# Down-projection and output projection with the weights as the standing operand, results turned by transposing DMAs

## The chip, the cores and the metric

The kernel runs on one core of one Trainium2 chip. The metric is the device time of one execution, in microseconds (us). The kernel before was run three times.

## What is computed

The kernel computes a layer norm, then two branches on its result, and joins them:

```python
xn = layernorm(x)                          # x: 2048 tokens x 640, bf16
q, k, v = split(xn @ wqkv)                 # 32 heads of 20
p = softmax(q @ k.T / sqrt(20))            # per head 2048 x 2048
s = concat_heads(p @ v) @ wo               # 640 x 640
h = sigmoid(xn @ w_gate) * (xn @ w_up)     # 640 -> 1728
g = silu(h @ w_down)                       # 1728 -> 640
out = x + s * g
```

## The kernel before

Tokens lie in 16 tiles of 128, or in four chunks (`c`) of 512. Heads go in eight groups of four (`g`). One group on one chunk of queries is a **block**; there are 32 blocks, and the last eight alternate groups 6 and 7 over chunks 0 to 3. A block has 64 score jobs, each of 128 keys by 512 queries for one head.

**Scores and exponentials.** A *fill* (line 889) multiplies two to four scores at once into PSUM: two into the pair `scA`, the others into single banks `bk` (three exist). ScalarE (ACT) takes the exponential of a pair (`pt`, 1024 wide) or of a bank (`px`, 512 wide), all through line 82. VectorE (DVE) computes exponentials too: an integer conversion out of a bank (`iv`, line 1327) and, for up to four together, three passes (`pb`, lines 1019, 1022, 1025). The attention sum (line 926) adds into `oacc`.

**The other matrix work** shares the three banks `bk`. It is cut into items of small steps, all through `cols` (line 473): four matmuls side by side, each with 32 columns of a standing operand. The gated unit's hidden values are `hT` (hidden x tokens). `mk_down` (line 719) multiplies them by `wd`: here `hT` stands and `wd` streams, so one item is 128 tokens by 320 outputs, 14 steps, eight items a chunk. ACT takes a tanh (`td`, 320 wide), DVE makes the silu (`gqs`, line 740), and for chunks 0 to 2 it is stored to DRAM (`gq_dram`, line 742); chunk 3 stays in SBUF (`gql`).

**The output projection** of chunks 0 to 2 (`mk_out`, line 773) multiplies the normalized attention `oU` by `wo`, `oU` standing: 128 tokens by 320, five steps, 24 items. DVE multiplies by the silu loaded again (`otmp`, line 795), GpSimd (POOL) adds `x` in two parts (line 800), and each token tile is stored (line 802). `load_out` (line 764) loads `x` and the silu into one of three areas of `xnT` that are free by then. Chunk 3 is finished in a tail written by hand (lines 1053 to 1136), whose first products (`early`, line 1045) may fill banks before attention is done.

**Normalization of a block** goes through DRAM: DVE copies `oacc` (line 959), SyncE (SP) issues `ld` and `lt`, DVE takes the reciprocal (`rt`, line 969), SP issues `rd` and four `rl`, POOL multiplies (lines 979, 984), SP issues the pieces of `oU` (lines 1009, 1011).

**What sets the order.** On PE, ACT, DVE and POOL the order is written by a planner, the loop from line 1231: it walks its own clock with fixed costs (0.2133 for a step 512 wide, 0.14 for one of `mk_down`), gives a fill to PE when ACT is about to run dry, and otherwise attention sums or steps of items, as far as their due times ask. DVE's exponentials are claimed at a fill, when DVE is not far behind and a bank is free; so the split of the 2048 jobs between ACT and DVE follows from the plan. POOL's adds wait in a list and are placed by `beat` beside DVE instructions that read PSUM. The order on SP's queue is not the planner's: it is settled when the program is built. All engines execute their queue in order.

Of the kernel before, what the change touches and what calls it, by code (L numbers as in the profile page):

```python
# [51 lines left out]
def kernel(  # L52
# [38 lines left out]
    persist = ctx.enter_context(tc.tile_pool(name="persist", bufs=1))  # L91
    wk = ctx.enter_context(tc.tile_pool(name="wk", bufs=2))

    gq_dram = dram.tile([S, D], FP32, name="gq_dram", tag="gqd", bufs=1)
# [373 lines left out]
    def mark(*e):  # L468
        return lambda t: ev_at.__setitem__(e, t)
# [194 lines left out]
    def mk_gu(c, kf, at):  # L664
        st = {}
        fs = fsz[kf]
        k2, ko = divmod(kf, 2)

        def alloc0():
            if (c, k2) not in wgu_tiles:  # L670
                load_wgu(c, k2)
            st["g"] = misc_ps()

        def alloc1():
            st["u"] = misc_ps()
            if ko == 0:
                n = c * NK2 + k2 + 1
                if n < NQC * NK2:
                    load_wgu(*divmod(n, NK2))

        def mm(key, i, kd):
            w = wgu_tiles[(c, k2)]
            cols(st[key], w[:, i, kd, ko * P:ko * P + P], xnT[:, c, kd, :], kd == 0, kd == KD - 1)

        def th():
            st["t"] = w2.tile([P, QC], BF16, tag="tnh", bufs=2, name="tnh")
            act_imm(st["t"][0:fs, :], st["g"][0:fs, :], ACT.Tanh, 0.5)

        def ev():
            return nc.vector.scalar_tensor_tensor(out=hT[0:fs, kf, :], in0=st["t"][0:fs, :], scalar=1.0,  # L690
                                                  in1=st["u"][0:fs, :], op0=ALU.add, op1=ALU.mult)

        def mm2(kd):
            cols(st["g"], wgu_tiles[(c, k2)][:, 0, kd, P:2 * P], xnT[:, c, kd, :], kd == 0, kd == KD - 1)

        def th2():
            st["t"] = w2.tile([P, QC], BF16, tag="tnh", bufs=2, name="tnh")
# [15 lines left out]
    def gq_last(t4):  # L713
        if len(gq_l) == t4 // 2:
            w = w2.tile([P, 2, KD, 2 * P], BF16, tag="wgu", bufs=2, name="gql")
            gq_l.append(w.rearrange("p i k f -> p (i k f)").bitcast(FP32))
        return gq_l[t4 // 2][:, t4 % 2 * D:(t4 % 2 + 1) * D]

    def mk_down(c, t4, h, at):
        st = {}  # L720
        tt = 4 * c + t4

        def alloc():
            st["ps"] = misc_ps()

        def mm(kf):
            cols(st["ps"][:, 0:HD], hT[:, kf, t4 * P:(t4 + 1) * P], wd[:, kf, h * HD:(h + 1) * HD],
                 kf == 0, kf == NFT - 1)

        def th():  # L730
            st["td"] = w2.tile([P, HD], BF16, tag="td", bufs=2, name="td")
            act_imm(st["td"], st["ps"][:, 0:HD], ACT.Tanh, 0.25)

        def ev():
            if c == NQC - 1:
                return nc.vector.scalar_tensor_tensor(out=gq_last(t4)[:, h * HD:(h + 1) * HD], in0=st["td"], scalar=1.0,
                                                      in1=st["ps"][:, 0:HD], op0=ALU.add, op1=ALU.mult)
            flush("o")
            gqs = w2.tile([P, HD], FP32, tag="gqs", bufs=3, name="gqs")
            ins = nc.vector.scalar_tensor_tensor(out=gqs, in0=st["td"], scalar=1.0, in1=st["ps"][:, 0:HD],  # L740
                                                 op0=ALU.add, op1=ALU.mult)
            nc.sync.dma_start(out=gq_dram[tt * P:(tt + 1) * P, h * HD:(h + 1) * HD], in_=gqs)
            return ins
        return Item([("PE", alloc, [(0.14, lambda kf=kf: mm(kf)) for kf in range(NFT)]),
                     ("ACT", 0.32, th), ("DVE", 0.40, ev, "free", mark("d", c, t4, h))], at, pre=[("h", c, kf) for kf in range(NFT)])


    FL, FG, FK = (NG - 1) * GC, (NG - 2) * GC, (KD - 1) * P
    FM = FG + 2 * DH
# [11 lines left out]
                                in1=rq.broadcast_to((P, n, GH, DH)), op=ALU.mult)  # L761
        return onq

    def load_out(tt):
        if tt in out_tiles:
            return
        o2 = xfl[:, tt % 3 * KD * QC:tt % 3 * KD * QC + 3 * D]
        flush("o")
        out_tiles[tt] = (o2[:, 0:D], o2[:, D:3 * D].bitcast(FP32))
        nc.sync.dma_start(out=out_tiles[tt][0], in_=x2[tt * P:(tt + 1) * P, :])  # L770
        nc.sync.dma_start(out=out_tiles[tt][1], in_=gq_dram[tt * P:(tt + 1) * P, :])

    def mk_out(tt, h, at):
        st = {}

        def alloc():
            if h == 0:
                load_out(tt)
                if (tt + 1) % 4:
                    load_out(tt + 1)  # L780
            st["ps"] = misc_ps()

        def mm(kd):
            hs = slice(h * HD, (h + 1) * HD)
            cols(st["ps"][:, 0:HD], oU[:, kd, tt * P:(tt + 1) * P], wo[:, kd, hs], kd == 0, kd == KD - 1)

        def ev():
            xr, gqr = out_tiles[tt]
            sl = slice(h * HD, (h + 1) * HD)
            while sum(x[1] == "o" for x in pool_q) > 2:  # L790
                x = next(x for x in pool_q if x[1] == "o")
                pool_q.remove(x)
                x[2]()
            tmp = w2.tile([P, HD], FP32, tag="gqs", bufs=3, name="otmp")
            ins = nc.vector.scalar_tensor_tensor(out=tmp, in0=st["ps"][:, 0:HD], scalar=0.25,
                                                 in1=gqr[:, sl], op0=ALU.mult, op1=ALU.mult)

            def part(i):
                cs = slice(h * HD + i * HD // 2, h * HD + (i + 1) * HD // 2)
                add = nc.gpsimd.tensor_tensor(out=xr[:, cs], in0=tmp[:, i * HD // 2:(i + 1) * HD // 2], in1=xr[:, cs], op=ALU.add)  # L800
                if h == 1 and i == 1:
                    nc.sync.dma_start(out=out2[tt * P:(tt + 1) * P, :], in_=xr)
                return add
            for i in range(2):
                pool_q.append((now + 0.6, "o", lambda i=i: part(i)))
            return ins
        return Item([("PE", alloc, [(0.136, lambda kd=kd: mm(kd)) for kd in range(KD)]),
                     ("DVE", 0.40, ev, "free", mark("o", tt, h))], at, need=ALT + 1 + 2 * (tt // 4),
                    pre=[("d", tt // 4, t4, i) for t4 in range(4) for i in range(2)] + [("h", 2, kf) for kf in range(NFT)] + (
                        [("o", tt - 2, 1)] if h == 0 and tt > 1 else []))  # L810
# [12 lines left out]
    for b in range(NBLK):  # L823
# [336 lines left out]
    with tc.manual_schedule(engines={ENG.PE, ENG.Activation, ENG.DVE, ENG.Pool}):  # L1160
# [70 lines left out]
        while len(chain_end) < len(chain) or fill or items or glu_items or any(it.i < len(it.ops) for it in active):  # L1231
# [298 lines left out]
```

## Time and profile before

| | |
|---|---|
| three runs | 802.97, 803.62, 803.87 us; median 803.62 |
| profiled execution | 803.38 us |
| its span | 801.6 us |
| ACT busy | 781.2 us |
| PE busy | 778.0 us |
| DVE busy | 770.2 us |
| POOL busy | 107.4 us |

The span is what the profiler records from the first to the last instruction; 1.8 us of the profiled execution lie around it. Instructions of one engine overlap: an ACT or DVE instruction is drawn with its start-up and drain, so its recorded length (1186 ns in the mean for a `pt`) is longer than the step from its start to the next one's start (about 0.91 us). For sums of work the step from start to start is what counts, and it is called **pitch** here. TensorE's granted clock is 1.00 from 20 us on to 795 us.

### The profile page before, as it was taken

How to read it: one execution, taken by the hardware profiler on the slowest of the kernel's cores; microseconds unless marked ns; L12 is line 12 of the kernel's file. 1: busy time of each engine (PE TensorE's matmuls, PEld its weight loads, DVE VectorE, ACT ScalarE, POOL GpSimd, SP SyncE). 2: the span in 40 equal slices, each digit the busy share in tenths (PEclk: the TensorE clock that was granted, in tenths of full speed). 3: DMA queues.
4: the chain of work that ended last, by engine and by line, in shares of the span. 5: the costliest groups of instructions: out<-in, count | busy, mean ns of one | idle time of the engine just before them, and what ended most of it. 6: DMA issues, size and time to landing. Idle time of an engine off the chain costs nothing.

```text
span 801.6 us, 25395 instructions
## 1 busy us (share of the span) xinstructions
PE 778.0 (97%) x10462; PEld 283.8 (35%) x10466; DVE 770.2 (96%) x1239; ACT 781.2 (97%) x991; POOL 107.4 (13%) x219
## 2 busy tenths in 40 slices
PE   7899999999999999999999999999999999999996
PEld 5523233333433323334332332334333333333333
DVE  7798999999999999989999999999999999999996
ACT  8799999999999999999999999999999999999993
POOL 7200000000000000000000010000000100502425
PEclk9999999999999999999999999999999999999999
DMA  5541213123122323222113132222311332331421
GB/s 162 147 117 48 70 40 86 53 67 80 46 69 61 78 67 100 51 60 68 49 47 97 50 86 76 80 75 60 96 40 58 91 90 53 105 104 34 131 62 62
DMA packets 91851, 60.47 MB, mean 75 GB/s; under 512 B 34891, under 2 KB 85627, under 8 KB 91735
## 3 DMA queue, kind: packets, MB, share of 16 engines
q1 hardware_dynamic: 91447, 58.52, 26.2%
q8 instruction: 82, 1.34, 0.7%
q14 instruction: 34, 0.28, 0.1%
q10 hardware_dynamic: 288, 0.33, 0.1%
HBM read 45.18 MB, written 11.09 MB: 70 GB/s over the span
## 4 chain that ended last, share of the span: by engine, by line
PE 47%; ACT 39%; DVE 6%; issue 5%; DMA 1%; POOL 1%; DVEq 0%; ACTq 0%; POOLq 0%; SPq 0%
ACT pt L82 31%; PE bk L473 20%; PE scA L889 14%; PE oacc L926 10%; ACT px L82 4%; DVE iv L1327 2%; ACT tnh L82 2%; DVE pb L1025 1%; PE bk L889 1%; ACT td L82 1%; DVE pb L1022 1%; PE tp L292 1%; DVE pb L1019 0%; DMA lt<-ld 0%; ACT aq L173 0%
## 5 line engine op out<-in xcount | busy, mean ns | idle before, releaser
L82 ACT ACTIVATE pt<-scA 128x1024 bf16<-128x1024 f32 (+1 forms) x709 | 707.8, 1186 | 1.2 <-PE scA L889 0.5
L1327 DVE TENSOR_SCALAR iv<-bk 128x512 int16<-128x512 f32 x500 | 331.5, 680 | 12.1 <-PE bk L889 9.6
L889 PE MATMUL scA<-q,kT 32*128 32x512 bf16 x1412 | 275.8, 382 | 8.7 <-ACT pt L82 3.3
L889 PE MATMUL bk<-q,kT 32*128 32x512 bf16 x636 | 207.3, 383 | 0.2 <-DVE iv L1327 0.2
L889 PEld LDWEIGHTS <-kT 32*128 32x128 bf16 x2048 | 88.4, 91 | 262.0 <-issue 250.7
L926 PE MATMUL oacc<-pt,v 128*21 128x512 bf16 x1412 | 178.6, 381 | 1.0 <-ACT pt L82 0.7
L926 PE MATMUL oacc<-pb,v 128*21 128x512 bf16 x1000 | 161.4, 382 | 0.0
L473 PE MATMUL bk<-xnT,wgu 128*32 128x512 bf16 x2160 | 157.3, 383 | 0.5 <-DVE iv L1327 0.2
L1025 DVE TENSOR_TENSOR pb<-iv,pb 128x2048 bf16<-128x2048 bf16 x125 | 152.0, 1216 | 0.7
L979 POOL TENSOR_TENSOR on_bf<-on,rl 128x128 bf16<-128x128 f32 x116 | 54.4, 473 | 626.7 <-DVE iv L1327 149.1
L82 ACT ACTIVATE px<-bk 128x512 bf16<-128x512 f32 x136 | 101.0, 760 | 1.7 <-POOL hT L1169 1.6
L1019 DVE TENSOR_SCALAR pb<-iv 128x2048 int16<-128x2048 int16 x125 | 86.9, 695 | 0.4
L473 PE MATMUL bk<-wd,hT 128*32 128x320 bf16 x1792 | 87.0, 302 | 0.1
L1022 DVE TENSOR_SCALAR pb<-iv 128x2048 int16<-128x2048 int16 x125 | 86.2, 690 | 0.0
L926 PEld LDWEIGHTS <-v 128*21 128x21 bf16 x2548 | 54.0, 91 | 76.2 <-issue 53.4
L473 PEld LDWEIGHTS <-wgu 128*32 128x32 bf16 x2160 | 44.5, 95 | 64.3 <-issue 45.9
L473 PEld LDWEIGHTS <-hT 128*32 128x32 bf16 x1792 | 37.5, 95 | 38.2 <-issue 32.7
L473 PE MATMUL bk<-xnT,wu 128*32 128x512 bf16 x640 | 48.4, 383 | 0.6 <-DVE iv L1327 0.2
L926 PE MATMUL oacc<-px,v 128*21 128x512 bf16 x136 | 46.7, 381 | 0.0
L82 ACT ACTIVATE tnh<-bk 128x512 bf16<-128x512 f32 (+1 forms) x56 | 43.2, 772 | 0.1
L690 DVE SCALAR_TENSOR_TENSOR hT<-tnh,bk 128x512 bf16<-128x512 bf16 x52 | 35.3, 679 | 1.0 <-PE bk L889 0.3
L800 POOL TENSOR_TENSOR xnT<-otmp,xnT 128x160 bf16<-128x160 f32 x48 | 28.2, 607 | 40.6 <-PE bk L889 15.9
(118 smaller groups left out, 410.5 us busy)
## 6 DMA issues: line engine op xcount, KB each, us to landing
rl<-rd SPq DMA_DIRECT2D x124, 64.0 KB
wgu<-in_B_w_gate_dram SPq DMA_DIRECT2D x24, 320.0 KB
wgu<-in_B_w_up_dram SPq DMA_DIRECT2D x24, 320.0 KB
gq_dram<-gqs SPq DMA_DIRECT2D x24, 160.0 KB
xnT<-gq_dram SPq DMA_DIRECT2D x12, 320.0 KB
xt<-in_A_x_dram SPq DMA_DIRECT2D x16, 160.0 KB
xnT<-in_A_x_dram SPq DMA_DIRECT2D x16, 160.0 KB
out_dram<-xnT SPq DMA_DIRECT2D x14, 160.0 KB
```

Of the source, the lines that this page charges most:

```text
L82: return nc.scalar.add_instruction(mybir.InstActivation(func=func, name=nc.get_next_instruction_name(), engine=ENG.Activation, ins=[nc.sca ...
L292: nc.tensor.transpose(out=tps[k][:, kd, :], in_=xns[k][:, kd * P:(kd + 1) * P], identity=ident)
L473: nc.tensor.matmul(out[j:j + 32, :], lhsT=lhsT[:, j:j + 32], rhs=rhs, start=start, stop=stop, tile_position=(0, j), skip_group_check=True)
L690: return nc.vector.scalar_tensor_tensor(out=hT[0:fs, kf, :], in0=st["t"][0:fs, :], scalar=1.0, in1=st["u"][0:fs, :], op0=ALU.add, op1=ALU. ...
L800: add = nc.gpsimd.tensor_tensor(out=xr[:, cs], in0=tmp[:, i * HD // 2:(i + 1) * HD // 2], in1=xr[:, cs], op=ALU.add)
L889: nc.tensor.matmul(dst, lhsT=kTs[gc_of(b)[0] % 2][32 * j:32 * j + 32, kt * P:(kt + 1) * P], rhs=qts[b % 3][32 * j:32 * j + 32, :], start=T ...
L926: nc.tensor.matmul(oacc[32 * j:32 * j + DH + 1, :], lhsT=lhsT, rhs=u["src"], start=first, stop=last, tile_position=(0, 32 * j), skip_group ...
L979: ins = nc.gpsimd.tensor_tensor(out=on_bf[:, cs], in0=on[:, cs], in1=rl[:, cs], op=ALU.mult)
L1019: ins = nc.vector.tensor_scalar(out=pb[:, 0, :, :].bitcast(I16), in0=iv, scalar1=0x7F80, scalar2=1, op0=ALU.bitwise_and, op1=ALU.bitwise_or)
L1022: ins = nc.vector.tensor_scalar(out=pb[:, 1, :, :].bitcast(I16), in0=iv, scalar1=0x007F, scalar2=0x3F00, op0=ALU.bitwise_and, op1=ALU.bitw ...
L1025: ins = nc.vector.tensor_tensor(out=pb[:, 1, :, :], in0=iv.bitcast(BF16), in1=pb[:, 1, :, :], op=ALU.mult)
L1327: beat(nc.vector.tensor_scalar(out=d["iv"][:, j, :], in0=bank[bk], scalar1=B_OFF, scalar2=0.0, op0=ALU.add, op1=ALU.max))
```

## The change

For chunks 0 to 2 the down-projection exchanges its operands: `wd` stands, `hT` streams, and one item is 128 outputs by 512 tokens (`mk_down_t`, 14 steps, five items a chunk). The output projection does the same with `wo` and `oU` (five items a chunk). Results are therefore transposed (outputs x tokens); the silu is stored and loaded in that form. `x` is brought in by a transposing DMA, the product and the sum are made in place, and the sum is turned back by a transposing DMA from SBUF to SBUF and then stored, 128 x 4 x 128. Both are put in the planner's list of timed events (2.5 and 8.5 after the last add). There are five areas in place of three, the adds are four parts of 128, the tanh tiles of both kinds share three buffers, and `gqs` has two. Chunk 3 and the tail keep the old form.

```diff
+NGQ, NTH, NOQ, NOT, T_YT, T_YO = 2, 3, 4, 5, 2.5, 8.5
...
+    def mk_down_t(c, e, at):
...
+        def mm(kf):
+            cols(st["ps"], wd[:, kf, e * P:(e + 1) * P], hT[:, kf, :], kf == 0, kf == NFT - 1)
...
+            act_imm(st["td"], st["ps"], ACT.Tanh, 0.25)
...
+            gqs = w2.tile([P, QC], FP32, tag="gqs", bufs=NGQ, name="gqs")
+            ins = nc.vector.scalar_tensor_tensor(out=gqs, in0=st["td"], scalar=1.0, in1=st["ps"],
+                                                 op0=ALU.add, op1=ALU.mult)
+            nc.sync.dma_start(out=g_rows(c, e), in_=gqs)
...
+        return Item([("PE", alloc, [(T_MM, lambda kf=kf: mm(kf)) for kf in range(NFT)]),
+                     ("ACT", 0.48, th), ("DVE", 0.60, ev, "free", mark("d", c, e))], at, pre=[("h", c, kf) for kf in range(NFT)])
...
+    def later(n, dt, f):
+        def go():
+            if go in unstored.get(n, ()):
+                unstored[n].remove(go)
+                f()
+        unstored.setdefault(n, []).append(go)
+        timed.append((now + dt, go))
...
-        nc.sync.dma_start(out=out_tiles[tt][0], in_=x2[tt * P:(tt + 1) * P, :])
-        nc.sync.dma_start(out=out_tiles[tt][1], in_=gq_dram[tt * P:(tt + 1) * P, :])
+        for go in list(unstored.get(n - NOT, ())):
+            go()
...
+        r = xfl[:, n % NOT * 3 * QC:(n % NOT + 1) * 3 * QC]
...
+        nc.sync.dma_start_transpose(out=out_tiles[n][0], in_=x2[c * QC:(c + 1) * QC, e * P:(e + 1) * P])
+        nc.sync.dma_start(out=out_tiles[n][1], in_=g_rows(c, e))
...
-            cols(st["ps"][:, 0:HD], oU[:, kd, tt * P:(tt + 1) * P], wo[:, kd, hs], kd == 0, kd == KD - 1)
+            cols(st["ps"], wo[:, kd, e * P:(e + 1) * P], oU[:, kd, c * QC:(c + 1) * QC], kd == 0, kd == KD - 1)
...
+            ins = nc.vector.scalar_tensor_tensor(out=gT, in0=st["ps"], scalar=0.25, in1=gT, op0=ALU.mult, op1=ALU.mult)
...
+                add = nc.gpsimd.tensor_tensor(out=xT[:, cs], in0=gT[:, cs], in1=xT[:, cs], op=ALU.add)
+                if i == NQC - 1:
+                    later(n, T_YT, lambda: nc.sync.dma_start_transpose(out=y, in_=xT))
+                    later(n, T_YO, lambda: nc.sync.dma_start(
+                        out=out2[c * QC:(c + 1) * QC, e * P:(e + 1) * P].rearrange("(t p) u -> p t u", p=P), in_=y))
```

More of the change, by code (lines that the diff above doesn't have):

```diff
@@ L92 @@
     wk = ctx.enter_context(tc.tile_pool(name="wk", bufs=2))
-    gq_dram = dram.tile([S, D], FP32, name="gq_dram", tag="gqd", bufs=1)
     NU = (HEADS - PG * GH) // UH
@@ L685, in th @@
         def th():
-            st["t"] = w2.tile([P, QC], BF16, tag="tnh", bufs=2, name="tnh")
+            st["t"] = w2.tile([P, QC], BF16, tag="tnh", bufs=NTH, name="tnh")
             act_imm(st["t"][0:fs, :], st["g"][0:fs, :], ACT.Tanh, 0.5)
@@ L696, in th2 @@
         def th2():
-            st["t"] = w2.tile([P, QC], BF16, tag="tnh", bufs=2, name="tnh")
+            st["t"] = w2.tile([P, QC], BF16, tag="tnh", bufs=NTH, name="tnh")
             act_imm(st["t"][fs:P, :], st["g"][0:fs, :], ACT.Tanh, 0.5)
@@ L730, in th @@
         def th():
-            st["td"] = w2.tile([P, HD], BF16, tag="td", bufs=2, name="td")
+            st["td"] = w2.tile([P, QC], BF16, tag="tnh", bufs=NTH, name="td")[:, 0:HD]
             act_imm(st["td"], st["ps"][:, 0:HD], ACT.Tanh, 0.25)
         def ev():
-            if c == NQC - 1:
-                return nc.vector.scalar_tensor_tensor(out=gq_last(t4)[:, h * HD:(h + 1) * HD], in0=st["td"], scalar=1.0,
-                                                      in1=st["ps"][:, 0:HD], op0=ALU.add, op1=ALU.mult)
@@ L738, in ev @@
[L738 to L743, printed above, removed]
+            return nc.vector.scalar_tensor_tensor(out=gq_last(t4)[:, h * HD:(h + 1) * HD], in0=st["td"], scalar=1.0,
+                                                  in1=st["ps"][:, 0:HD], op0=ALU.add, op1=ALU.mult)
@@ L744, in mk_down, with g_rows, alloc, th @@
         return Item([("PE", alloc, [(0.14, lambda kf=kf: mm(kf)) for kf in range(NFT)]),
                      ("ACT", 0.32, th), ("DVE", 0.40, ev, "free", mark("d", c, t4, h))], at, pre=[("h", c, kf) for kf in range(NFT)])
+    gqT = dram.tile([NQC * D, QC], FP32, name="gqT", tag="gqd", bufs=1)
+    def g_rows(c, e):
+        return gqT[c * D + e * P:c * D + (e + 1) * P, :]
+    def mk_down_t(c, e, at):
+        st = {}
+        def alloc():
+            st["ps"] = misc_ps()
+        def mm(kf):
+            cols(st["ps"], wd[:, kf, e * P:(e + 1) * P], hT[:, kf, :], kf == 0, kf == NFT - 1)
+        def th():
+            st["td"] = w2.tile([P, QC], BF16, tag="tnh", bufs=NTH, name="td")
+            act_imm(st["td"], st["ps"], ACT.Tanh, 0.25)
+        def ev():
+            flush("o")
+            gqs = w2.tile([P, QC], FP32, tag="gqs", bufs=NGQ, name="gqs")
+            ins = nc.vector.scalar_tensor_tensor(out=gqs, in0=st["td"], scalar=1.0, in1=st["ps"],
+                                                 op0=ALU.add, op1=ALU.mult)
+            nc.sync.dma_start(out=g_rows(c, e), in_=gqs)
+            return ins
+        return Item([("PE", alloc, [(T_MM, lambda kf=kf: mm(kf)) for kf in range(NFT)]),
+                     ("ACT", 0.48, th), ("DVE", 0.60, ev, "free", mark("d", c, e))], at, pre=[("h", c, kf) for kf in range(NFT)])
@@ L762, in div_scale, with load_out, mk_out @@
         return onq
-    def load_out(tt):
-        if tt in out_tiles:
+    unstored = {}
+    def later(n, dt, f):
[5 more added lines that the diff above has]
+        timed.append((now + dt, go))
+    def load_out(n):
+        if n in out_tiles:
             return
-        o2 = xfl[:, tt % 3 * KD * QC:tt % 3 * KD * QC + 3 * D]
+        for go in list(unstored.get(n - NOT, ())):
+            go()
+        c, e = divmod(n, KD)
+        r = xfl[:, n % NOT * 3 * QC:(n % NOT + 1) * 3 * QC]
         flush("o")
-        out_tiles[tt] = (o2[:, 0:D], o2[:, D:3 * D].bitcast(FP32))
-        nc.sync.dma_start(out=out_tiles[tt][0], in_=x2[tt * P:(tt + 1) * P, :])
-        nc.sync.dma_start(out=out_tiles[tt][1], in_=gq_dram[tt * P:(tt + 1) * P, :])
-    def mk_out(tt, h, at):
+        out_tiles[n] = r[:, 0:QC], r[:, QC:3 * QC].bitcast(FP32), r[:, QC:2 * QC].rearrange("p (t u) -> p t u", u=P)
+        nc.sync.dma_start_transpose(out=out_tiles[n][0], in_=x2[c * QC:(c + 1) * QC, e * P:(e + 1) * P])
+        nc.sync.dma_start(out=out_tiles[n][1], in_=g_rows(c, e))
+    def mk_out(c, e, at):
         st = {}
+        n = c * KD + e
         def alloc():
[L777 to L780, printed above, removed]
+            load_out(n)
+            if e < KD - 1:
+                load_out(n + 1)
             st["ps"] = misc_ps()
         def mm(kd):
-            hs = slice(h * HD, (h + 1) * HD)
-            cols(st["ps"][:, 0:HD], oU[:, kd, tt * P:(tt + 1) * P], wo[:, kd, hs], kd == 0, kd == KD - 1)
+            cols(st["ps"], wo[:, kd, e * P:(e + 1) * P], oU[:, kd, c * QC:(c + 1) * QC], kd == 0, kd == KD - 1)
         def ev():
-            xr, gqr = out_tiles[tt]
-            sl = slice(h * HD, (h + 1) * HD)
-            while sum(x[1] == "o" for x in pool_q) > 2:
+            xT, gT, y = out_tiles[n]
+            while sum(x[1] == "o" for x in pool_q) > NOQ:
                 x = next(x for x in pool_q if x[1] == "o")
@@ L793, in ev @@
                 x[2]()
-            tmp = w2.tile([P, HD], FP32, tag="gqs", bufs=3, name="otmp")
-            ins = nc.vector.scalar_tensor_tensor(out=tmp, in0=st["ps"][:, 0:HD], scalar=0.25,
-                                                 in1=gqr[:, sl], op0=ALU.mult, op1=ALU.mult)
+            ins = nc.vector.scalar_tensor_tensor(out=gT, in0=st["ps"], scalar=0.25, in1=gT, op0=ALU.mult, op1=ALU.mult)
             def part(i):
[L799 to L802, printed above, removed]
+                cs = slice(i * P, (i + 1) * P)
+                add = nc.gpsimd.tensor_tensor(out=xT[:, cs], in0=gT[:, cs], in1=xT[:, cs], op=ALU.add)
[3 more added lines that the diff above has]
+                        out=out2[c * QC:(c + 1) * QC, e * P:(e + 1) * P].rearrange("(t p) u -> p t u", p=P), in_=y))
                 return add
-            for i in range(2):
+            for i in range(NQC):
                 pool_q.append((now + 0.6, "o", lambda i=i: part(i)))
             return ins
[L807 to L810, printed above, removed]
+        return Item([("PE", alloc, [(T_MM, lambda kd=kd: mm(kd)) for kd in range(KD)]),
+                     ("DVE", 0.60, ev, "free", mark("o", n))], at, need=ALT + 1 + 2 * c,
+                    pre=[("d", c, i) for i in range(KD)] + [("h", 2, kf) for kf in range(NFT)] + ([("o", n + 1 - NOT)] if n + 1 >= NOT else []))
     glu = []
@@ L816 @@
             glu.append(lambda at, c=c, kf=kf: mk_gu(c, kf, at))
+        if c < NQC - 1:
+            for e in range(KD):
+                glu.append(lambda at, c=c, e=e: [mk_down_t(c, e, at)])
+            continue
         for h in range(2):
@@ L840 @@
         if b >= ALT + 2:
-            n = (b - ALT - 2) * 4
-            for i in range(n, n + 4):
-                mk.append(lambda at, t=i // 2, h=i % 2: [mk_out(t, h, at)])
+            n = (b - ALT - 2) * KD // 2
+            for i in range(n, (b - ALT - 1) * KD // 2):
+                mk.append(lambda at, i=i: [mk_out(*divmod(i, KD), at)])
         for i, f in enumerate(mk):
@@ L1497 @@
         assert not items and not glu_items and not any(it.i < len(it.ops) for it in active)
+        flush("n", "o")
         for tm in timed:
```

## The prediction

> **What bounds the kernel now.** I read the busy times first, then who ACT waited for, then instructions in order of time.
>
> ```profile
> PE 778.0 (97%) x10462; PEld 283.8 (35%) x10466; DVE 770.2 (96%) x1239; ACT 781.2 (97%) x991; POOL 107.4 (13%) x219
> ```
>
> Three engines are nearly full, so shares do not tell which one binds. The stages do; columns are PE, weight load, DVE, ACT and POOL busy, clock, DMA share, GB/s:
>
> ```profile
> 200.00:300.00 100.00, 99.04 (x1431) 34.35 (x1428) 98.34 (x158) 100.00 (x129) 9.10 (x20) 1.00 0.23 64
> 600.00:700.00 100.00, 99.57 (x1407) 33.55 (x1408) 98.91 (x154) 99.96 (x126) 17.58 (x33) 1.00 0.28 78
> 780.00:795.00 15.00, 13.88 (x153) 5.85 (x151) 11.72 (x20) 9.38 (x14) 9.26 (x11) 1.00 0.12 40
> ```
>
> ACT has no idle time from the first exponential (30.2 us) to the last 15 us. Its waits for PE between exponentials (us in total, times, longest) are:
>
> ```profile
> ACT pt L82 <- PE scA L889: 0.5, 1, 0.5
> ACT pt L82 <- PE bk L889: 0.3, 2, 0.2
> ```
>
> That is 0.8 us in 750. So the time is ACT's work plus what the ends add, and each edit is priced by what it puts on or takes off ACT. Pitches come from ACT in order of time:
>
> ```profile
> 202.52 0.51 ACT L82 ACTIVATE td<-bk 128x320 bf16<-128x320 f32 x1
> 202.84 5.69 ACT L82 ACTIVATE pt<-scA 128x1024 bf16<-128x1024 f32 x6
> 208.26 0.59 ACT L82 ACTIVATE td<-bk 128x320 bf16<-128x320 f32 x1
> 208.58 0.77 ACT L82 ACTIVATE px<-bk 128x512 bf16<-128x512 f32 x1
> 209.06 1.21 ACT L82 ACTIVATE pt<-scA 128x1024 bf16<-128x1024 f32 x1
> ```
>
> Start to start: a tanh 320 wide takes 0.32 (202.52 to 202.84), six `pt` 5.42 or 0.90 each, a `px` 0.48 (208.58 to 209.06). A tanh 512 wide takes the same 0.48 (44.40 to 44.88).
>
> **The change, part by part.**
>
> *ACT.* The order of the built program shows 24 tanh of 320 replaced by 15 of 512: 24 x 0.32 = 7.68 off, 15 x 0.48 = 7.20 on. But the planner's split moves too: DVE has 497 `iv` where it had 500, and ACT gets those three jobs, as 137 `px` for 136 and 8 half-width `pt` for 6 (703 full ones in both): 3 x 0.48 = 1.44 on. Net **+0.96 us**, with nothing beside it, since ACT has no gaps to hide it in.
>
> *PE.* Down-projection and output projection were 336 + 120 steps of 320 columns and are 210 + 75 of 512: 145,920 columns in both. In the chain of waits runs of 8, 12 and 16 matmuls on `bk` (line 473, 320 wide) last 0.39, 0.52 and 0.66, so a step of four is 0.135; on `oacc` (512 wide) 0.54, 0.76 and 0.97, a step of 0.215. 456 x 0.135 = 61.6 against 285 x 0.215 = 61.3. The planner books 0.14 and 0.136 for the old steps and 0.2133 for the new, so most of what it saves was never there. Changes between kinds of matmul, which cost some 0.11 each by the same rows, are 1441 for 1442. PE: -0.4 us, off the path, since ACT ends last in every stage: 0. If PE were the bound instead, it would be a gain of that size.
>
> *DVE.* Off: 24 `gqs` at 0.39 (203.65 to 204.04) and 24 `otmp` at 0.40, three `iv` at 0.60, one set of passes four wide for one of one (0.60 + 0.60 + 1.13 less about 0.8, an estimate from a quarter of these): about 22.3. On: 30 products 512 wide; the nearest row, the hidden values' product (line 690, 512 wide from PSUM), has a pitch of 0.60: 18.0. Net -4.3 us, hidden behind ACT: 0. It could count only where DVE makes PE or ACT late.
>
> *The last 10 us* are such a place:
>
> ```profile
> 780.82 1.57 DVE L1019 TENSOR_SCALAR pb<-iv 128x2048 int16<-128x2048 int16 x1
> 782.31 0.97 DVE L1022 TENSOR_SCALAR pb<-iv 128x2048 int16<-128x2048 int16 x1
> 783.32 1.39 DVE L1025 TENSOR_TENSOR pb<-iv,pb 128x2048 bf16<-128x2048 bf16 x1
> 784.63 0.48 DVE L795 SCALAR_TENSOR_TENSOR otmp<-bk,xnT 128x320 f32<-128x320 f32 x1
> ```
>
> The pass that takes 695 ns in the mean takes 1.57 while POOL multiplies and adds (780.57 to 785.1). `otmp` is late, its bank with it, and PE waits 0.84 us at 785.17 before line 473 goes on; ACT between 779.87 and 787.58 holds 6.87 us of pitches in 7.71, a gap of **0.84**. The old out items run until two fills before the last; in the new order five fills follow the last out item, so I count the gap as gone: -0.84. If POOL is beside the passes there as before, it stays. The Trainium skill (GPSIMD Engine Reference, section "Key points") says GpSimd shares its SBUF interfaces with VectorE and contends with instructions in a 2-port mode or with two SBUF inputs. The row agrees (1.57 against 0.69), and it speaks against the change: 60 adds of 128 for 48 of 160 do not lower POOL's time, so by the rule the 0.84 would stay.
>
> *POOL.* 60 adds at the 473 ns of the 128 x 128 multiply (line 979) are 28.4 us, for 28.2. 0.
>
> *SP and the DMAs.* SP gains 15 transposing loads for 12 plain ones, and 15 transposing DMAs inside SBUF before 15 stores; `gq_dram` stores and loads go from 36 to 30. No trace here shows a transposing DMA. Issue: between the shortest plain one (0.32, `rd`) and the longest (2.73, the second `wd` load). Issue to completion: between 1.4 (729.09 to 730.51, `rd` until `rl` may go) and 2.8 (the longest such wait on `rd`). I take 0.75, the issue of an `oU` piece, which moves many short rows as these do, and 2.0. In the built order the first five loads stand far ahead, and each later one about a chunk ahead, so DVE's product should not wait. What stands behind a waiting store on SP is the normalization. Before, for block 30:
>
> ```profile
> 769.97 0.53 SPq L961 DMA_DIRECT2D ld<-on  x1
> 771.67 0.33 SPq L963 DMA_DIRECT2D lt<-ld  x1
> ...
> 775.06 0.32 SPq L971 DMA_DIRECT2D rd<-rt  x1
> ...
> 776.89 1.77 SPq L974 DMA_DIRECT2D rl<-rd  x4
> 781.87 3.03 SPq L1011 DMA_DIRECT2D oU<-on_bf  x4
> ```
>
> In the new order there stand a transpose and its store (which waits for it) between `lt` and `rd`, a transpose between `rd` and `rl`, and a transpose and two stores between `rl` and `oU`. With 0.75 and 2.0: transpose done 774.75, store 775.15, `rd` 775.5, `rl` 777.0 to 778.8, POOL's product ends 781.9, the last store issues at 781.9, `oU` goes at 781.9 as before. Cost 0. The cover is POOL's product, which waits for `rl` and takes 1.3 us; with the upper bounds it is gone (below). The Trainium skill's page "Advanced Engine Details and Errata" states under "X-Bar Transpose (TRN2)" that transposing DMAs are as fast as regular ones, and in its table under "DGE: Hardware vs Software" that the hardware path, used here, is the worse one for them; no run shows either. By the first the sum is unchanged, by the second the queue rival gains.
>
> *Sum:* 803.38 + 0.96 - 0.84 = 803.5 for the profiled execution. That stood 0.24 below the median; to the median, **803.7**.
>
> **The rivals.** (1) *SP's queue sets the end.* With 2.7 and 2.8: transpose issued 774.7, done 777.5, store 777.9, `rd` 778.3, second transpose 781.0, `rl` to 782.75, third transpose 785.45, stores 788.7, `oU` issued by 791.7 in place of 784.9, landed about 1.9 later, 793.6. In the built order the first product that needs it now stands between the last attention sum (790.26) and the transposes of the tail, about 790.8; before it stood at 792.58. So 4.0 us of added delay are free, 6.8 leave 2.8 on the end. The same at block 29, whose `oU` the out items of chunk 2 need, can starve PE about 1 us. Time 803.7 + 2.8 = 806.5, with that 807.5. For it: five transposes in 20 us, each followed by a store that waits. Against: SP idles between 732.2 and 739.5. Slower; it decides once issue and completion together exceed about 4.5.
> (2) *Only the added ACT work counts*, and the gap stays: 803.62 + 0.96 = 804.6.
> (3) *The plan runs tighter*: `pt` pitches average 0.92 against the best 0.90, some 11 us of small lateness of PE, 3 of it in the 200 us of stages that change. Half of that and 0.5 of the drain after the last exponential (789.1 to 790.26) off: 803.7 - 2.0 = 801.7. For it: DVE has 4.3 us less. Against: lateness is no greater in these stages than elsewhere.
> (4) *The change doesn't do what it says*: the PE saving exists in the planner's costs alone. That is my own reading and part of the forecast.
> (5) *DVE in order stalls on the silu or PE on `oU`* in each of three out stages, about 1.5 us each, the longest such idle time before (`iv` on PE, 1.5): 803.7 + 4.5 = 808.2.
>
> **How the numbers follow.** Forecast with (2), both within 802.0 to 805.2: 0.44. Rival 3: 0.20. Rival 1: 0.27. Rival 5: 0.09. Within 0.2% means within 1.6 us, about what this measurement can tell from no change. Faster 0.21 (rival 3 and an edge), same 0.44, slower 0.35. Range: from just under rival 3 (801.5) to the end of rival 1 (807.5); it leaves out rival 5 and tails of the others.
>
> **What would show it.** ACT with no gap until the end and 0.96 us more pitch; the last out item several fills ahead of the last exponential and no 1.57 pass there; `oU` of block 30 issued before about 786; transposing DMAs that hold SP under 1 us each. Wrong: issue times of 2 us or more on SP, DVE's `rt` or PE's line 473 waiting on a DMA after 680 us, or an ACT sum that falls.

## The result, and the profile after

The changed kernel takes **822.73 us** (median of five runs, 822.46 to 823.18); the kernel before, run five times on the same chip, 803.83 (802.97 to 804.11). The ratio is 1.0232, 95% interval 1.0221 to 1.0244: 2.3% slower, where 803.7 was forecast and the range ended at 807.5.

Busy times on the page of the changed kernel (span 821.4 us; line numbers are now those of the changed kernel):

```profile
PE 783.0 (95%) x9779; PEld 265.8 (32%) x9779; DVE 767.8 (93%) x1218; ACT 782.9 (95%) x985; POOL 111.4 (14%) x231
```

ACT's work grew by 1.7 us of recorded length, but its idle time (span less busy) went from 20.4 to 38.5. So the loss is a wait, and three views say where. The waits (us in total, times, longest):

```profile
DVE rt L1004 <- DMA lt<-ld: 17.6, 2, 9.4
DVE iv L1362 <- PE bk L924: 15.3, 28, 1.6
```

```profile
ACT pt L83 <- PE bk L924: 10.8, 4, 9.7
ACT td L83 <- PE bk L473: 6.9, 1, 6.9
```

```profile
PE bk L924 <- DVE iv L1362: 15.3, 2, 8.3
```

DVE stands twice at the reciprocal of a normalization, PE stands for the banks that DVE should have emptied behind it, ACT stands for PE's scores: the same two stalls, 17.6 us together, seen from three engines. Before, `rt` waited 1.5 us in the whole run. DVE's instructions in order of time have the two places, blocks 27 and 29 (the bracket gives the idle time ahead and its releaser):

```profile
702.84 0.69 DVE L994 COPY on<-oacc 128x512 f32<-128x512 f32 x1
...
721.38 0.25 DVE L1004 RECIPROCAL rt<-lt 128x16 f32<-128x16 f32 x1 [8.22 <-DMA lt<-ld]
...
757.65 0.67 DVE L994 COPY on<-oacc 128x512 f32<-128x512 f32 x1
...
772.44 0.25 DVE L1004 RECIPROCAL rt<-lt 128x16 f32<-128x16 f32 x1 [9.39 <-DMA lt<-ld]
```

From the copy to the reciprocal 18.5 and 14.8 us pass. Before, block 27's copy stood at 702.32 and its reciprocal at 712.60, with no wait. SP's queue shows what lies between. Changed kernel:

```profile
704.87 0.74 SPq L644 DMA_DIRECT2D q<-qD  x2
705.67 0.49 SPq L645 DMA_DIRECT2D q<-bD  x1
706.25 0.41 SPq L833 DMA_DIRECT2D out_dram<-xnT  x1
706.71 3.10 SPq L1044 DMA_DIRECT2D oU<-on_bf  x4
709.86 0.48 SPq L805 DMA_DIRECT2D xnT<-gqT  x1
710.39 1.17 SPq L804 DMA_TRANSPOSE xnT<-in_A_x_dram  x1
711.67 0.51 SPq L805 DMA_DIRECT2D xnT<-gqT  x1
712.23 2.58 SPq L1073 DMA_DIRECT2D xnT<-in_A_x_dram  x4
714.90 1.23 SPq L832 DMA_TRANSPOSE xnT<-xnT  x1
716.22 0.56 SPq L996 DMA_DIRECT2D ld<-on  x1
717.80 0.41 SPq L833 DMA_DIRECT2D out_dram<-xnT  x1
718.31 1.24 SPq L832 DMA_TRANSPOSE xnT<-xnT  x1
719.64 0.52 SPq L998 DMA_DIRECT2D lt<-ld  x1
```

Kernel before:

```profile
703.07 0.37 SPq L770 DMA_DIRECT2D xnT<-in_A_x_dram  x1
703.53 0.38 SPq L802 DMA_DIRECT2D out_dram<-xnT  x1
704.01 0.55 SPq L961 DMA_DIRECT2D ld<-on  x1
704.65 2.12 SPq L1038 DMA_DIRECT2D xnT<-in_A_x_dram  x4
706.88 0.37 SPq L963 DMA_DIRECT2D lt<-ld  x1
```

`ld` could go at 703.5 and goes at 716.2. In that time SP hardly waits; it issues, one DMA after another, with the tail's four loads of `x` now ahead of `ld`. Then the store of a tile waits until 717.80 for its transpose, with a second transpose behind it and `lt` behind that. The load follows from the issues of SP's queue, added up one by one (a merged row such as `x4` also spans the waits between its DMAs). From 690 us to the end of the run issuing takes 43.5 us of 112 before and **82.1 of 131** after, 31.6 of it in 25 transposing DMAs; in the first 30 of these us, where block 27 is normalized, 16.2 before and 25.7 after. Such sums from 690 us on are given below for other kernels too.

The stall also cools TensorE. Columns are PE, weight load, DVE, ACT and POOL busy, granted clock, DMA share, GB/s, for each stall and the stretch behind it:

```profile
714.00:722.00 8.00, 1.24 (x16) 0.43 (x16) 0.62 (x2) 2.64 (x3) 0.00 (x0) 0.70 0.55 141
722.00:730.00 8.00, 7.77 (x98) 2.47 (x98) 6.89 (x12) 4.68 (x7) 0.00 (x0) 0.66 0.46 115
764.00:773.00 9.00, 1.01 (x16) 0.25 (x15) 0.56 (x2) 2.64 (x4) 0.16 (x1) 0.74 0.52 121
773.00:778.00 5.00, 4.71 (x43) 1.07 (x42) 4.72 (x8) 1.50 (x2) 1.11 (x3) 0.50 0.52 138
```

The clock is 0.66 and 0.50 behind the gaps, and 1.00 in the same stage before. The Trainium skill (TensorE: Matmul & The Clock Gate, section "Part 1: The HAM clock gate") states that an idle window of about 3.4 us halves the clock; PE's gaps here are 7.0 and 8.3 us, and the 0.50 behind the second agrees. This is a consequence of the stall, not its cause.

### The profile page after: what moved, and what is told of

It is laid out like the page before. It is cut to its first block, busy times and chain, and to the rows that moved or that the text cites. A ratio compares the mean times of both kernels' runs of the same rounds, so it can differ in the third digit from the quotient of the medians.

```text
span 821.4 us, 24042 instructions
## 1 busy us (share of the span) xinstructions
PE 783.0 (95%) x9779; PEld 265.8 (32%) x9779; DVE 767.8 (93%) x1218; ACT 782.9 (95%) x985; POOL 111.4 (14%) x231
## 4 chain that ended last, share of the span: by engine, by line
ACT 49%; PE 35%; issue 7%; DVE 4%; DMA 2%; SPq 1%; POOL 0%; DVEq 0%; ACTq 0%; POOLq 0%
ACT pt L83 40%; PE bk L473 14%; PE scA L924 11%; PE oacc L961 7%; ACT px L83 5%; ACT tnh L83 3%; DVE iv L1362 1%; DMA xnT<-xnT 1%; ACT td L83 1%; PE bk L924 1%; PE bk L654 1%; DVE pb L1060 1%; PE tp L292 1%; ACT aq L173 1%; PE scrap L398 0%
## 5 line engine op out<-in xcount | busy, mean ns | idle before, releaser
L83 ACT ACTIVATE pt<-scA 128x1024 bf16<-128x1024 f32 x711 | 700.5, 1165 | 12.4 <-PE bk L924 10.8
L924 PE MATMUL bk<-q,kT 32*128 32x512 bf16 x634 | 210.4, 385 | 15.4 <-DVE iv L1362 15.3
L961 PE MATMUL oacc<-pt,v 128*21 128x512 bf16 x1414 | 181.4, 383 | 0.5 <-ACT pt L83 0.5
L961 PE MATMUL oacc<-pb,v 128*21 128x512 bf16 x994 | 167.3, 384 | 0.7 <-DVE on L994 0.5
L1060 DVE TENSOR_TENSOR pb<-iv,pb 128x2048 bf16<-128x2048 bf16 (+1 forms) x125 | 151.8, 1214 | 0.7
L1054 DVE TENSOR_SCALAR pb<-iv 128x2048 int16<-128x2048 int16 (+1 forms) x125 | 87.1, 697 | 0.7
L1057 DVE TENSOR_SCALAR pb<-iv 128x2048 int16<-128x2048 int16 (+1 forms) x125 | 87.0, 696 | 0.0
L473 PE MATMUL bk<-hT,wd 128*32 128x512 bf16 x840 | 62.7, 384 | 0.3 <-DVE hT L701 0.3
L830 POOL TENSOR_TENSOR xnT<-xnT 128x128 bf16<-128x128 f32 x60 | 34.4, 594 | 60.1 <-DVE xnT L826 28.7
L83 ACT ACTIVATE tnh<-bk 128x512 bf16<-128x512 f32 (+1 forms) x56 | 40.7, 727 | 0.1
L654 PE MATMUL bk<-wv,xnT 128*128 128x160 bf16 x280 | 29.1, 235 | 0.6 <-ACT px L83 0.6
```

The lines of the kernel that those rows point to most:

```text
L83: return nc.scalar.add_instruction(mybir.InstActivation(func=func, name=nc.get_next_instruction_name(), engine=ENG.Activation, ins=[nc.sca ...
L473: nc.tensor.matmul(out[j:j + 32, :], lhsT=lhsT[:, j:j + 32], rhs=rhs, start=start, stop=stop, tile_position=(0, j), skip_group_check=True)
L654: nc.tensor.matmul(st["ps"][:, i * 2 * GC:(i + 1) * 2 * GC], lhsT=xn_tok(tts[i], kd), rhs=wvs[pr][:, kd, :], start=(kd == 0), stop=(kd == ...
L830: add = nc.gpsimd.tensor_tensor(out=xT[:, cs], in0=gT[:, cs], in1=xT[:, cs], op=ALU.add)
L924: nc.tensor.matmul(dst, lhsT=kTs[gc_of(b)[0] % 2][32 * j:32 * j + 32, kt * P:(kt + 1) * P], rhs=qts[b % 3][32 * j:32 * j + 32, :], start=T ...
L961: nc.tensor.matmul(oacc[32 * j:32 * j + DH + 1, :], lhsT=lhsT, rhs=u["src"], start=first, stop=last, tile_position=(0, 32 * j), skip_group ...
```

## The experiments

**Theory:** SP's in-order queue is overloaded in the output projection's stages, so that `ld` and `lt` come late, DVE stands at `rt`, and everything stands behind DVE. **Rivals,** in several forms: the transposed items themselves cost the time, or the lateness returns elsewhere whatever is done for `ld` and `lt`, or the transposing DMAs slow the small transfers themselves. Times are medians; the kernel before gave 803.7 to 804.0 beside each of them.

**1. Plain DMAs of the same bytes in place of all 30 transposing ones.**

```diff
-nc.sync.dma_start_transpose(out=out_tiles[n][0], in_=x2[c * QC:(c + 1) * QC, e * P:(e + 1) * P])
+nc.sync.dma_start(out=out_tiles[n][0].rearrange("p (t u) -> p t u", u=P), in_=x2[...].rearrange("(t p) u -> p t u", p=P))
-nc.sync.dma_start_transpose(out=y, in_=xT)
+nc.sync.dma_start(out=y, in_=xT.rearrange("p (t u) -> p t u", u=P))
```

> The changed kernel with its 30 transposing DMAs replaced by plain DMAs between the same places, of the same bytes (rows then lie unturned, so the output is not the reference's); PE, ACT and DVE keep their orders to the instruction. Theory (SyncE's queue: a transposing DMA holds it 1.2 us, the normalization's ld and lt stand behind, and DVE's reciprocal rt waits in order): a plain DMA holds SP about 0.5, so 30 x 0.7 = 21 us of issue are gone, the two waits of rt (8.2 and 9.4 us) fall under 2 us together, and the time is 803 to 807. Rival A (the form with the weights standing costs the time on PE or ACT itself): stays at 820 to 823. Rival B (what costs is the round trip from SBUF to SBUF and the store that waits for it, turned or not): 812 to 820.

Measured: 813.41 us, ratio 1.0119 (1.0104 to 1.0134). Summary rows of the line that turns the result, changed kernel and this one (ns: shortest, median, longest):

```profile
L832 SPq DMA_TRANSPOSE xnT<-xnT x15: 1188/1231/1918, 691.0 to 811.5; - x15
```

```profile
L832 SPq DMA_DIRECT2D xnT<-xnT x15: 470/522/974, 690.5 to 800.0; - x15
```

```profile
DVE rt L1004 <- DMA lt<-ld: 8.3, 3, 4.3
```

Each transposing DMA holds SP 0.7 us longer than a plain one. Without that, half of the stall and half of the loss go (SP issues 61.9 us from 690 us on). The theory in its simple form, that the issue time is all, falls short by the other half; the time lies in the range of rival B, the round trip inside SBUF with a store that waits for it. Experiment 7 keeps that round trip, with `ld` and `lt` out of its way, and loses nothing: it costs only through what stands behind it.

**2. `ld` and `lt` issued by GpSimd in the last eight blocks.**

```diff
-nc.sync.dma_start(out=ld, ...)
+(nc.gpsimd if b >= ALT else nc.sync).dma_start(out=ld, ...)
-nc.sync.dma_start(out=lt, ...)
+(nc.gpsimd if b >= ALT else nc.sync).dma_start(out=lt, ...)
```

> The changed kernel with ld and lt of the last eight blocks issued by GpSimd instead of SyncE; nothing else moves. Theory (the loss is ld and lt standing behind the backlog on SP): rt waits under 3 us in all, time 804 to 808, a little above the plain one because rd, rl and oU still go through SP. Rival A (weights standing): 820 to 823. Rival C (transposing DMAs delay the small transfers on the DMA rings themselves, not in SP's queue): rt still waits 10 us or more, time above 813.

Measured: 815.54 us, 1.0143 (1.0127 to 1.016). `rt` still waits 5.0 us, once, and PE now waits 3.5 for `oU`: `rd`, `rl` and `oU` are still late on SP. The wait of `rt` is at block 28, whose copy ended at 728.14. GpSimd's rows:

```profile
732.65 2.10 POOL L1014 TENSOR_TENSOR on_bf<-on,rl 128x128 bf16<-128x128 f32 x4 [23.27 <-DMA q<-qD]
734.70 0.59 POOL L996 DMA_DIRECT2D ld<-on  x1
```

`ld` stood on GpSimd behind the product of block 27, and that came late through SP: `rt` of block 27 is at 714.10, but SP issued `rd` only at 726.10 and `rl` from 728.50. Taking two DMAs out of a full queue moves the wait on. Rival C names a time above 813 us, which came out, and a wait of 10 us or more, which did not. Nor do the rows show slower small transfers: from the issue of `lt` to `rt` 1.7 us pass in the changed kernel (719.64 to 721.38), and 1.6 before at block 28 (727.25 to 728.81).

**3. The down projection's part alone**, with the old output projection and no transposing DMA: `load_out` and `mk_out` are those of before, reading `gqT` as rows of 640.

```diff
-        nc.sync.dma_start_transpose(out=out_tiles[n][0], in_=x2[c * QC:(c + 1) * QC, e * P:(e + 1) * P])
-        nc.sync.dma_start(out=out_tiles[n][1], in_=g_rows(c, e))
+        nc.sync.dma_start(out=out_tiles[tt][0], in_=x2[tt * P:(tt + 1) * P, :])
+        nc.sync.dma_start(out=out_tiles[tt][1], in_=gqT.rearrange("a b -> (a b)").rearrange("(s d) -> s d", d=D)[tt * P:(tt + 1) * P, :])
```

> The down-projection of chunks 0 to 2 transposed, the output projection of before, without any transposing DMA. It reads the silu's bytes as they lie, so the values are in the wrong places and the output is not the reference's. Theory: no backlog, no wait of rt beyond that of before (1.5 us), time 802.5 to 805. Rival A: the 15 of 19.5 us that go with 840 of 1140 transposed matmuls would show here, 815 to 820.

Measured: 809.41 us, 1.007 (1.0055 to 1.0085). The theory missed, and the rival's range too: 5.7 us are lost with no transposing DMA, and SP issues only 46.6 us from 690 us on. `rt` waits 5.0 us, 3.7 of it at block 29.

**4. SP's queue put in the planner's order too.**

```diff
-    with tc.manual_schedule(engines={ENG.PE, ENG.Activation, ENG.DVE, ENG.Pool}):
+    with tc.manual_schedule(engines={ENG.PE, ENG.Activation, ENG.DVE, ENG.Pool, ENG.SP}):
```

> The changed kernel with SyncE's queue in the planner's order too (every DMA stands where the planner issues it), the other engines' orders unchanged to the instruction. ld then stands right behind the copy of oacc, ahead of the tail's four loads, but still behind the transposes issued before it, and lt right behind ld. Theory, part one (order: ld stands in the wrong place): rt waits less than 5 us, time 804 to 812. Theory, part two (load: SP has more to issue than it has time): the wait moves to other places (DVE waiting for the silu, SP waiting for POOL's adds at the head of the queue) and the time is 812 to 825.

Measured: 832.62 us, 1.0358 (1.0343 to 1.0374). `rt`'s wait falls to 1.2 us, but DVE's product waits 11.6 us for its silu, and near the start PE waits for a weight:

```profile
47.39 1.47 PE L473 MATMUL bk<-xnT,wqk 128*32 128x512 bf16 x12 [8.53 <-POOL wqk L128]
```

That start is another loss: in the first 100 us ACT is busy 9.9 us less than in the changed kernel, and the time is 9.9 us longer. From 690 us on ACT is idle for 28.5 us here and for 29.9 in the changed kernel. So with the wait of `rt` nearly gone the stage costs as much as before it: this order moves the wait and does not get the load through. Other orders were not tried.

**5. The reciprocal of blocks 27 and 29 placed later.**

```diff
-(T_LT if norm_pending[0] < NBLK - 4 else T_L2)
+(T_LT if norm_pending[0] < NBLK - 5 else 18.0 if norm_pending[0] == NBLK - 5 else 14.0 if norm_pending[0] == NBLK - 3 else T_L2)
```

> The changed kernel with one thing altered: DVE's reciprocal rt of blocks 27 and 29 is placed 18.0 and 14.0 us after the copy instead of 9.0 and 4.5; no DMA is touched. Theory (the cost is that DVE, which works in order, stands at rt for a DMA that SP issues late): the waits of rt for lt fall from 17.6 us to under 3, and 805 to 812 us come out, not 803.7, since the rows of block 27 reach the output projection that much later and the rest of it has to be fitted in at the end. Rival B (DVE's stand is only where the lateness shows; the late rows themselves hold up the output projection): the wait moves to PE or DVE at the output projection, 818 to 824 us.

Measured: 826.69 us, 1.0286 (1.027 to 1.0302), slower than the changed kernel and above both ranges. DVE in order of time:

```profile
722.35 0.25 DVE L1004 RECIPROCAL rt<-lt 128x16 f32<-128x16 f32 x1 [1.20 <-DMA lt<-ld]
...
743.75 0.25 DVE L1004 RECIPROCAL rt<-lt 128x16 f32<-128x16 f32 x1 [6.82 <-DMA lt<-ld]
...
797.27 0.25 DVE L1004 RECIPROCAL rt<-lt 128x16 f32<-128x16 f32 x1 [14.08 <-DMA lt<-ld]
```

At block 27 the wait is down to 1.20 and at block 29 it is gone, and blocks 28 and 30 have it, 22.1 us in all; PE waits 10.8 for `oU` besides. So moving the place where DVE stands does not remove the lateness; it comes out at the next block and at `oU`. How much of that is the queue's and how much comes from `rd`, `rl` and `oU` being later by this very edit was not separated.

**6. The kernel before, with 26 transposing DMAs added to SP that nobody needs.** This is the test whether the load alone is enough.

```diff
+        nc.sync.dma_start_transpose(out=o2[:, 0:QC], in_=x2[0:QC, 0:P])
         nc.sync.dma_start(out=out_tiles[tt][0], in_=x2[tt * P:(tt + 1) * P, :])
...
+                    sp = xfl[:, tt % 3 * KD * QC + 3 * D:tt % 3 * KD * QC + 3 * D + QC]
+                    nc.sync.dma_start_transpose(out=sp.rearrange("p (t u) -> p t u", u=P), in_=xr[:, 0:QC])
                     nc.sync.dma_start(out=out2[tt * P:(tt + 1) * P, :], in_=xr)
```

> The kernel before, its projections untouched, with 26 transposing DMAs added to SP that nobody needs: for each output tile of the first three chunks, one of 512 rows x 128 columns of x into the tile's area ahead of its load of x (which waits for it), and one of 128 x 512 from the finished tile into a spare part of the same area ahead of the store (which does not wait for it). Theory (SP's load alone does it): waits of rt for lt of 5 to 18 us in place of 1.5, and 809 to 822 us. Rival B (the transposed form on PE, DVE and ACT costs the time, SP's lateness is by the way): 803 to 806 us, rt's waits under 4 us.

The count in that text is off: 12 tiles get two each, 24.

Measured: **822.37 us**, 1.0228 (1.0198 to 1.0258), the changed kernel's time to within the intervals, with the old projections untouched. SP issues 74.2 us from 690 us on, 26.3 of it in the 20 added DMAs that fall there. DVE's waits and its instructions in order of time:

```profile
DVE rt L972 <- DMA lt<-ld: 13.8, 3, 6.9
```

```profile
719.25 0.25 DVE L972 RECIPROCAL rt<-lt 128x16 f32<-128x16 f32 x1 [6.52 <-DMA lt<-ld]
...
768.78 0.25 DVE L972 RECIPROCAL rt<-lt 128x16 f32<-128x16 f32 x1 [6.88 <-DMA lt<-ld]
```

The stalls are in the same two blocks. Load on SP, by issues and by the loads of `x` that wait for the added DMAs, is sufficient.

**7. Experiments 1 and 2 together**; the edits are those two diffs.

> Both halves of the first experiments together: the 30 transposing DMAs are plain ones of the same bytes (so the output is not the reference's), and the two DMAs that carry the denominators out and back are issued by GpSimd in the last eight blocks. Theory (two causes in one queue, the issue time and the place in the order, which add up): rt's waits under 3 us and 803 to 808 us. Rival B (whatever is taken off that wait comes back as another one, as when the two DMAs alone were moved): 810 to 815 us, with a wait at oU, at the silu product or at rl in its place.

Measured: **803.83 us**, 0.9998 (0.9989 to 1.0008). Page and waits:

```profile
PE 777.6 (97%) x9779; PEld 264.8 (33%) x9779; DVE 768.1 (96%) x1218; ACT 782.9 (97%) x985; POOL 121.4 (15%) x245
```

```profile
DVE rt L1004 <- DMA lt<-ld: 0.3, 1, 0.3
```

Everything of the change is in this kernel but the turning, and the loss is gone; SP still issues 56.7 us from 690 us on, against 43.5 before the change. One half saved 9.3 us, the other 7.2, both together 18.9, more than the sum of 16.5: each alone left part of the lateness standing. POOL's busy time grew by 10.0 us for 14 DMAs.

**8. The silu loads and the stores issued by GpSimd**, the transposing DMAs left on SP.

```diff
-nc.sync.dma_start(out=out_tiles[n][1], in_=g_rows(c, e))
+nc.gpsimd.dma_start(out=out_tiles[n][1], in_=g_rows(c, e))
-nc.sync.dma_start(out=out2[...], in_=y)
+nc.gpsimd.dma_start(out=out2[...], in_=y)
```

> The changed kernel with its transposing DMAs as they are on SP, but each output tile's silu load and store issued by GpSimd: SP loses two issues of about 0.5 us for each tile and each store's wait of about 2 us for its transpose. Theory (SP's queue is the resource): in the last 130 us SP is relieved of about 10 x (0.5 + 0.5) of issue and 8.5 us of waits, so rt's waits fall to under 8 us and 806 to 814 us come out. Rival B (the load moves to the next in-order queue: GpSimd's adds stand behind stores that wait for their transposes): waits of DVE or SP for GpSimd grow by over 8 us, 815 to 826 us.

Measured: 822.86 us, 1.0243 (1.0225 to 1.0261). `rt` waits 4.4 us only and SP issues 67.0 us, yet nothing is won: DVE waits 3.8 us for the silu, ACT 13.1 for banks `bk` in the last 250 us, and SP's loads of `x` wait 9.1 us for earlier transposes. ACT's idle time is 36.2 us, spread in pieces. The rival's time was met, but not by the one wait it named; how the pieces hang together was not followed further. Moving the transposes themselves was not tried: the Trainium skill (DMA: Bandwidth & Descriptors, section "DMA Transpose (X-bar)") has plain transposing DMAs on SP and ACT alone, and ACT is the engine that binds.

**9. Control for the edit of 2 and 7:** the kernel before with `ld` and `lt` on GpSimd, by the diff of experiment 2.

> The kernel before with only this altered: the two DMAs that carry the denominators out and back are issued by GpSimd in the last eight blocks. It is the control for the kernels that have this edit. Theory (before, SP was late by only 1.5 us at rt, and ACT, the bound, did not feel it): 803.0 to 804.5 us. Rival B (the edit is a gain of its own, so that the even result of the plain copies with this edit hides a cost of the new order): 800 to 802.5 us.

Measured: 803.95 us, 1.0002 (0.9993 to 1.0011). The edit by itself is worth nothing, so the even result of 7 hides no cost.

**10. The down projection's part alone** (experiment 3) **with the diff of experiment 2.**

> The down projection's part alone (which cost 5.7 us; the silu's bytes lie in other places than the reference's, so that the output is not its), with the same two DMAs issued by GpSimd. Theory (its loss was the place of these DMAs in SP's order, no transposing DMA being there): rt's waits under 1 us, 803.2 to 805.5 us. Rival B (the transposed down projection costs something else, on ACT or PE): 807 to 810 us, with ACT's or PE's waits as they were.

Measured: 808.61 us, 1.0057 (1.0043 to 1.0071): the theory missed. The time lies in the rival's range, but `rt` still waits 4.5 us, so this does not show a cost on ACT or PE. GpSimd's rows show that this was no freedom from queues either:

```profile
745.98 1.83 POOL L822 TENSOR_TENSOR xnT<-xnT 128x160 bf16<-128x160 f32 x4
747.75 0.59 POOL L987 DMA_DIRECT2D ld<-on  x1
751.27 0.57 POOL L989 DMA_DIRECT2D lt<-ld  x1 [2.93 <-DMA ld<-on]
```

The copy ended at 746.7; `ld` stood behind an add, `lt` could go 3.5 us after `ld`, and `rt` waited 3.6 us at 754.92. The plan allows 4.5 us from copy to reciprocal in the last blocks; here 8 were needed.

**11. The changed kernel with SP relieved and the turning kept:** the transposes of `x` go one to a block, in blocks 2 to 16, into DRAM, and the output projection loads them by plain DMAs; `ld` and `lt` as in 2.

```diff
+    def pre_x(n):
...
+        d = nc.sync.dma_start_transpose(out=t, in_=x2[c * QC:(c + 1) * QC, e * P:(e + 1) * P])
+        tc.add_manual_dep(d.ins, dve_ins[0].ins.name, SYNC, reason="after this block")
+        nc.sync.dma_start(out=xTd[c * D + e * P:c * D + (e + 1) * P, :], in_=t)
...
-        nc.sync.dma_start_transpose(out=out_tiles[n][0], in_=x2[...])
+        nc.sync.dma_start(out=out_tiles[n][0], in_=xTd[c * D + e * P:c * D + (e + 1) * P, :])
...
+        if 2 <= b < 2 + 3 * KD:
+            pre_x(b - 2)
```

> The changed kernel as it must be to compute the right thing, with SP relieved in the loaded stage: the 15 transposes of x are issued one for each block in blocks 2 to 16, into DRAM, so that the output projection loads x already transposed by a plain DMA (0.5 us of SP in place of 1.2); the transposes of the result stay; the two DMAs of the denominators are issued by GpSimd in the last eight blocks. Theory (the loss follows SP's load in the last 130 us; plain copies for both kinds of transposes gave 803.8 with this edit, none gave 815.5): half of it remains at most, 804.5 to 810 us, waits at oU or the silu product under 4 us. Rival B (the transposes of the result, each with a store behind it that waits for it, are the larger part): 811 to 816 us.

Measured: 811.3 us, 1.0103 (1.008 to 1.0125). With 15 transposes in the stage in place of 25, SP issues 70.0 us of 119, and of experiment 2's loss 4.2 us go and 7.5 stay. The transposes of the result are the larger part, as the rival had it. It is not the waiting store alone: experiment 7 has the same stores waiting for plain DMAs and loses nothing. Where exactly the 7.5 us arise was not followed.

**12. The down projection's part alone, all DMAs on SP, block 29's reciprocal planned 8.5 us after the copy** instead of 4.5.

```diff
-(T_LT if norm_pending[0] < NBLK - 4 else T_L2)
+(T_LT if norm_pending[0] < NBLK - 4 else 8.5 if norm_pending[0] == NBLK - 3 else T_L2)
```

> The down projection's part alone (its output is not the reference's, since the silu's bytes lie in other places), all DMAs on SP as in its first run, with DVE's reciprocal of block 29 placed 8.5 us after the copy in place of 4.5. In the first run DVE stood 3.7 us there, and the kernel took 809.4 us. Theory (4.5 us was already too short before, where rt waited 0.67 us; the planned place is what the late DMA runs into, and there is room behind it): no wait of rt at block 29 above 0.5 us, 804.5 to 807 us. Rival B (the place is not free either: what stands behind the normalization then comes late, as with 14 and 18 us in the changed kernel): 808.5 to 812 us.

Measured: 805.79 us, 1.0025 (1.0014 to 1.0037). Two thirds of that part's loss were this one wait against a planned time that was too short; `rt`'s waits are 1.4 us in all. Here, where SP's queue is not full, the later place is free; in experiment 5 it was not. Why `rt` waited longer at block 29 in experiment 3 than before is in part in SP's rows there. The copy ended at 747.82, and `ld` stood until 751.32 behind pieces of `oU` of block 28, which go out between 747.18 and 753.40; before, they were out by 743.83. Why the plan has them later stays open.

None of these beats the kernel before.

## Why the prediction was wrong

**The step that failed is the one on SP and the DMAs**, "Cost 0". It was worked out for block 30 alone, from an idle queue at 770 us, although its own text said "What stands behind a waiting store on SP is the normalization". It counted 30 transposing DMAs and never added up what they hold of SP, it asked for the delay of `oU` and not for that of `ld` and `lt`, and so it missed that DVE, in its order, would stand at `rt`. The loss is at blocks 27 and 29, where the output tiles of a whole chunk pass through SP.

- *Sizes.* Issue was taken as 0.75 us and measures 1.18 (`x`) and 1.23 (result); completion was taken as 2.0 and measures 1.7 behind the issue in the rows above, 1.1 where it is shortest. One transposing DMA thus takes 2.9 us from the start of its issue to the store that waits for it (714.90 to 717.80; 2.3 to 4.0 over the nine that a store waited for), where 2.75 was assumed; a plain one of the same bytes takes 2.0 (experiment 1, 784.72 to 786.71). The time of one was about right; what it holds of SP was not, and the number of them was not multiplied by it: 25 x 1.23 is 31 us in a stage of some 112 in which SP already issued for 43.5.
- *Rival 1* named the right queue, but its condition (issue and completion above 4.5 us) was not met, and the loss came all the same. It priced a delay of the last `oU` on the end; the stretch behind attention is no longer than before (11.2 us from 810.2, 11.3 from 790.3). "SP idles between 732.2 and 739.5" was the argument against it: one free stretch between two crowded ones.
- *The sign* was listed: "DVE's `rt` ... waiting on a DMA after 680 us". Before, `rt` waited 0.79 us at block 28 and 0.67 at block 29, that is, its planned place had no slack left there. At block 27 there was some: `lt` was issued at 706.88 and `rt` came at 712.60, about 4 us of slack, an estimate with the 1.6 us that `lt` took at block 28. The rows were in the trace: beyond that slack, DVE pays for a later `lt`.
- *The skill's rules on transposing DMAs.* The Trainium skill (Advanced Engine Details and Errata, section "X-Bar Transpose (TRN2)") states that they are as fast as regular ones. Here the shortest time from the start of the issue to the waiting store is 2.3 us for a transposing DMA and 2.0 for a plain one, and SP is held 2.4 times as long by the issue (1231 against 522 ns); the measurement decides. By the table of the same page of the Trainium skill under "DGE: Hardware vs Software" the hardware path is the worse one for them; no run here shows it, since the other path was not run.
- *The rest of the sum* is borne out as a whole by experiment 7: 803.83 against the 803.7 forecast, with nothing of the change missing but the turning. PE is 777.6 us against 778.0, which fits the -0.4 forecast but does not prove it: experiment 9, with the matmuls of before, has 779.1. So the planner's saving was on paper (rival 4). DVE is 2.1 us less in recorded lengths, where -4.3 in pitches was forecast, and hidden. ACT has the three extra jobs (137 `px`, 8 half-width `pt`). In the last 10 us a pass beside POOL still takes long (2.45 at 778.22), and ACT's gap there is 0.37 us instead of 0.84, so that one was only half gone. Single terms below 1 us can't be told apart in the time, and rival 2's 804.6 is at the edge of the interval (803.1 to 804.6), so it is not ruled out.
- *Rival 5* (in-order stalls of DVE and PE) had the right mechanism on the wrong DMAs, 4.5 us in size; *rival 3* (a tighter plan, 801.7) is not borne out by experiment 7.

## What to carry to other kernels

Add up a queue's issue time by stage, before and after a change, as for an engine: here SP went from 16.2 to 25.7 us in 30, and its urgent DMAs stood behind the rest. The sum is a warning and not a price: experiment 2 issues 80.5 us from 690 us on and takes 815.5, experiment 8 issues 67.0 and takes 822.9, so what stands ahead of the urgent DMAs counts as well. Look first for instructions of a busy engine that already wait a little for a DMA; there the slack is spent. And when a wait has two causes in one queue, remove both before judging either.

## What the runs showed of the hardware

A transposing DMA of 128 x 512 bf16 holds SP's queue for 1.18 us (from DRAM) or 1.23 (SBUF to SBUF; both medians in the changed kernel), a plain one of the same bytes inside SBUF for 0.52 (experiment 1). From the start of the issue to the store that waits for it 2.3 us pass at the least, with the plain one 2.0. A DMA issued by GpSimd holds it for 0.57 to 0.59 us (experiment 7). Two gaps of 7.0 and 8.3 us on PE were followed by a mean granted clock of 0.66 and 0.50 over the next 8 and 5 us.
